# A sigmoid of one column behind the sines, and a new table of the order, in a recurrence with a gated long convolution

## The chip, the cores and the metric

The kernel runs on one core of one Trainium2 chip. The time is device microseconds of that core for one launch. Times of the kernel before are from three runs; engine times are from one profiled execution of it. Engines: TensorE (PE) multiplies matrices into PSUM, VectorE (DVE) and ScalarE (ACT) read PSUM and compute, GpSimd (POOL) computes on SBUF, SyncE (SP) issues all DMAs of this kernel from one queue. In this text an instruction takes "so many us" as the profile has it.

## The reference

Two stages, one behind the other (batch B = 4, sequence S = 6272, width D = 256, all float32):

```python
# stage 1: a gated linear recurrence along the sequence
sig = 1 / (1 + exp(-f_logit));  f = lower_bound + (1 - lower_bound) * sig
for t in range(S):
    h = f[:, t] * h + (1 - f[:, t]) * x[:, t];  y[:, t] = h
# stage 2: projection, circular convolution of one part along the sequence, gating
proj = y @ w_proj;  x1, x2, x3 = proj split in three of width D
x2_conv = irfft(rfft(x2, axis=1) * rfft(filter, axis=0), axis=1)
out = (x1 * x2_conv * x3) @ w_out
```

## The kernel before

The convolution of length 6272 = 49 * 128 is done by matrix products with small tables of sines and cosines, which the kernel makes itself.

**Prologue.** `prepare` (line 435) makes the tables: index patterns on POOL, arguments on DVE ("args", line 541), one sine over 520 columns on ACT ("sin", line 542), and copies of its parts into the tables D1, FT, VA, VB, ID. The filter (13 groups of up to four rows of 128 x 256, group 12 with one row) is loaded ("ff", line 604), cast ("fr", line 609), rotated on PE ("rot", line 615) and copied out of PSUM ("f2", line 618). Then for 16 units u come two first products ("FF1", line 630) with their copies "afs" (line 635), a small copy "mX" on POOL (line 639), the second product ("FF2", line 648), its scaled copy "hw" (line 653), and the store of the filter's spectrum to DRAM ("hst", line 657). "warm" (line 582) is a product of the identity that PE runs 24 times between the rotations; its results aren't used. "pad" (line 598, ACT in both orders) fills gaps of f2 with two copies. "W" (lines 477 to 487) scales and casts the weights.

**Recurrence** (`hgrn`, line 318), per batch in 13 chunks c of 512 steps (chunk 12 has 128): loads of f_logit and x, "sig" (the sigmoid, ACT, line 334), "u" (x times sigmoid, POOL, line 336), then for each half of the width: transposes "su" on PE (line 348), "f" (ACT line 361 or DVE line 363), "scan" (DVE, line 369) and, for the first half of the sequence, a copy "wrap" (line 377).

**Spectrum** (`spectrum`, line 827): `phase_p` (line 691) projects x2: 13 products "P" (line 700; group 12 has one row, the others four) and 13 copies "x2" out of PSUM to the tile X2, on ACT or DVE (line 703). All of them must be there before the transform "F1" (line 713) of any of the 16 units, whose copy is "A". "mini" and "zm" treat frequency zero; per unit follow "F2" (line 775), the load of the spectrum "H", two products with it per unit ("prod" on DVE straight from PSUM, called MUL in the table of the order, or a copy followed by "pm" on POOL, line 807), the inverse "I2" (line 817) and its copy "Th".

**Gate** (`gate`, line 384): products "x13" (line 397), copies "xs" and the product of the two, on DVE from PSUM (MUL, line 418) or on POOL ("z", line 427).

**Output** (`phase_o`, line 867): 13 groups of "I1" (PE, line 880), "y" (DVE, line 886), "proj" (PE, line 898), "o" (copy to SBUF, ACT or DVE, line 911) and "store" (SP, line 912). The tile ys has two halves, used in turn by even and odd groups.

The recurrence of batch b + 1 overlaps spectrum, gate and output of batch b.

**What sets the order.** The calls of `op` (line 77) only list operations, with the engines that may run each and an assumed length on each (its `cost`), for instance `either(n)` (line 296): 0.045 + n/1200 us on ACT and 0.07 + n/960 on DVE. The table ORDER (line 125) holds three characters per operation: its number, its engine and its PSUM bank. `emit` (line 108) walks the table and issues each operation on the engine named, so ORDER fixes the sequence on every engine and on the DMA queue, the engine of each operation that has a choice, and the banks. At run time each engine works through its own sequence, and semaphores hold it where data or a buffer isn't ready. SP is one such sequence: a load whose buffer isn't free holds back whatever stands behind it. ACT needs a table for the function it evaluates; the load of a table appears in the trace as an instruction of its own (ACT_TABLE_LOAD), ahead of the first activation that needs another table: at the start (line 280), before the sine (line 542) and before the first sigmoid (line 334).

Of the kernel before, what the change touches and what calls it, by code (L numbers as in the profile page):

```python
# [10 lines left out]
F32 = mybir.dt.float32  # L11
# [4 lines left out]
AF = mybir.ActivationFunctionType  # L16
# [45 lines left out]
class Plan:  # L62
# [63 lines left out]
    "A+gA2gAygA6gBCgBGgAAYAOYAgQAbQAiQAZQAaQAcQAeQAfQAdQAnQAhQAkQAqQAmQA3AABIACIA4QArSAPIAvSAzYARIA0SA7YA/IA1KAjUBAUA8WAp"  # L126
    "SBHYDngBWgBOgBKgAQAAXSAlTBegDmgBSgA5IBBMAxABIQBDYAtTBEUBJAA9GAUYBPIBQQBRAAVAAYCATIBFMBXYBagBigDpgDqgEBgD1gAoTADgD2gE"
    "NgDogECgEOgEZgEagElgAwTBLYAsTBMQBYUBZEAWIBTIBNIBfYBUSBgWBbIBcQBhGBjYASYAuUBVKBdABkUBlMDrADsYBoQBmUBpIBvSBwKBnEBtWEDA"
    "BuGBqYBxYAEYBrUB2SB4QBsMD3AByWDtUB5IB3KBzGB/QB9SB6YCAAB+CD4YCBYEEYB7WDxQDuMDvMB8GExgCCSDyIDzICDCEPACNUD5WCISD9QD6GCO"
    "MCJKD7OD+ACGUCHED/ICPSEFUCLWCQCCYSEGMEbACMGCWQEQYCKYCRYCZKCfWCSSCXAEnACTCEzAEHMEJQERUCgOEmgE7gEygCdWCeGEKICbSCcCEcYE"  # L130
    "SMELIETMCaYEoYAFgEVWEdQCmSEhUEWGE9AEXOEeACnCEfICoWEiEEpSCpGEjMCiQEqCCrWCjAErKChYCsGEtUE0YE1QEuMEvME8gFFgE2ACvSCtWAIY"
    "CwCCuGEIYCqYE+YAHYAJYEUYALYAMYAKYCxYFHAEMYE4SC2WCEgFPgAGgFGgFIYFZgFQgB0gFjgCFgFagCUgFkgE3ICyUE5CCzEC3OE6KE/QC9WC/UFC"
    "SFRADAEC+OFAIFbAFDKC4WDCUFBIC5GDDEC6YDBYFJWFEKDPQFKGFMUFLODQAFNEC7SJSQJTRC8CDIWDGSFOMJUAJVBDHKD0YFSYDJOJXQFtgFlAJZAA"
    "NYCVgFugDFgCkgDEgFTUFWSB1gFUMFVMDNWFXCFcYFmYEAYDOGDLQDMAFdWFYKDSUFeGFgQDWSDTEDKYDwYD8YDRYFfODYUFhAFvADXKDZEFnWDfSDdU"
    "FiIFoGDgCFwYEgYEkYEYYFqQFxSFpOFyKFzKDeEFrADiUJYWJcXF0SDjEDbUFsIF1KF2KJdQMtgJhRF+gEsYDcEDVgMugG2gF4gMVgMhgClgC0gDUgMi"
    "gF5gC1gDkgGkgDlgF3gGtgEwYJWYG/gMWgF6YF7YJauGQSGRCJePJfoJjJGSUGAWGBOGTEGUQMvAGVIGWSGGUGXCGHMGEWGIQMjAGJAMXAGFOGOUGCSG"
    "KQGLAGPMGDKGMUGNEJiWGYQJmXJnSGZIJkuJoHJpqDaYJlYMkYDhYGaQGbAGgWGeUGfEGcSGdCGlQGhOGnoF8WF9GJrUJsVJtMGpoGiSJwQJxUHIWJyA"
    "GjKGuQJzsG3SGyoGwoJuFHJGGzYGxYGmYGoYJvYGqYGrUG7qG5CHKWGsEJ1RJ2SJ3BJ4qHAUG4YGvYHLGHSgG0QG8YG6YHCsHEsHBYMYYJ6THOWG1AJ7"
    "SHPGJ8DJ9qHMQJ/UG9WKAVKBMHNAHTSHQQKEUG+GHXCHVqKCtHFYHWYHYYHDYKGEHGWKFTKJSHkgHbgH2UKHrHRIHHGHcWKLCHtgHlQIAgH3EHpAHguH"
    "euKDYHhYHdYHUYHZSHmYHnoHoYHqYJgYHfYH4UHaCH5EKKRKOXHiSH6UHjKKQHKMBHuWH7EH8QH9AHrSHwuHyuHsCH+QIBUH/IMZSIDEIFsIKQMaCMdW"  # L140
    "IOAMbKHvYJqYMwYKNYMeGHxYISgIJgICYHzYIEYH0UIGYIPYILYKPRH1EMfOIkSIHUITWIMoKRpIVuIlCIIEIcSIXGMlUMpQKTXMmMIgCIeCMqAIYYIU"
    "YINYIQSMrIMnMKVHKUWKYXKWuM5gF/gIbgIugM6gNFgIhYKIYIfYJ+YIdYNGgIWYI3gIRCIZSIvQIxoM7AKaHIaCImUInEKZXIoSKbvIpCKdWKeQIzoK"
    "fGIqUKiXIyYM8YIrEIiSKjRKkPKgoKlpIjCNHAIsUI4WItMI8uMxSM1QMyCIwYI9YI5YI6GI0YNIYKmYKnUKoVKsXKtWI7YMzKKpEM2AKqtKuHM9SM3I"
    "I1UJAgKvGM+CNBWKwYKXYNRgI2EM/KJBQJJgNSgKxUNJSKyVNCGJDAJFoKzENTANKCNDOK0tK2UI+QNNWI/ANLKK4ENOGNdgNegNngNogK3VK7QK8UK5"
    "tK9AJKSNPOK+sNfALAVLBQLFRJOqJbYJPYJEYKhYJ5YJLYJCYNUYLCFLDoJMCLEYJ0YKcYJGYNgYNVWLHBNWGNXOJHUJIENZSNhQLGUNaCNpANbKLKVN"
    "kWLLSLIsNiALMFNlGJNYNqYNjILNCJQULPTLQSJRENmOLRDLSqLJYK6YLOYKSYK/YLZUNxgNygN8gN7gLUQNrWNuSOGgOFgNsGNvCNQYNzAKrYMgYMcY"
    "N0YK1YLTYLaMLbULcELVILWQLjUNwKNtOLkMLXALeSRxWLfKN1QN9ARzGRyXN4UN2AN+YN3IR0HN5EOHAN6MLtSLlWLmGLgQLuKLoUN/WOCSLhALpMOA"
    "GOPgLdgOQgLYgLigOZgOagOBOLvQODCLwALqULrEM0YORAOEKOIYNMYM4YOSYNYYMsYMoYL3WL4OLyQOJSOMULzIONEL5WL0QOKCL6GL1AOOMOLKL8UL"
    "9MOTWR2QOWSR3ROUGObAOVOOXCR5BR4AOcYNcYNAYNEYL+UOYKOdWOgQOeGOfOMBSMGWOhAU1gLsgVBgLngU0gVMgLxgVNgL2gVAgL7gL/EOiIMCKMHO"
    "MAgO3QO4AOnUO1SOtWOrQOoEOuGOsAU2AOlUOmEVOAO2KO5WOjQOvSOwCO6OOxWOkIOzUO0MOyGOpSO7WMDQO8OOqCVCAO9SO+CMEIMLWPDUMMOPBQPE"  # L150
    "EO/SPCIMIWPACMQUPHQMRMPPSPJoMJGVPYU3YVDYR1YMFgPFUMNWPTCPGMPLoR7QMOGPnUR8TPoEPKYPQYPIYPMYPUYPNWPYYR6YR9IPRqPXQPZoPboP"
    "cYPSYPaYR+DPOGPfUPrSPhEPsCPVWSAQSBUSDMPjsSCAPpSPWGPdQPyWPqCPxgP6gP0uP2uPiYPgYP1YR/YP3YSFUPeAQDgMKgQfgQMgSEYPkYPtSSGV"
    "PuCPlQSIFP7SSHMPmAPvWPwOP/qSKVSLUP9CSMFU4WQVQSNsU5GQWAU6OP8YPzYP4SU8UU9MU+MQEQQIoP+YSJYP5CQNWQGAQRGQHYQJYQAYQBSQCCSP"
    "QSQXQXUSRAQZSSUQQYESWAQaCSSvQPuSVRSZXQbUSXpQSYSaQSeWSfRQcESbPSgOScoQFYQOYQQYSYYQKSQdWQeOQgUShBVEQVIWVZgQogVYgQisQLCQ"
# [24 lines left out]
    "9UgCKgFQglWf+EgDSgmGgHoi5Ui6Vi+QgEKgJogNSgRqgPqgQYizYgSYgIYi4YgKYi7Ei8FgGYi9YgOYgVWjAAdQUgXGdREgLQgMAi/WgnUgoEjDTjFD"
    "gYYgZujBugTQjESjGqgeYgaYgdUgfsggYgWYgbWgwSgUAghEgvggyqg0qgiYgzYgcGgpQg4ggqAjIUjJVgrWgjQjNSjOTjKEgsGjLtgkAjPKgtWg5Ugu"  # L180
# [12 lines left out]
def kernel(  # L193
# [33 lines left out]
    A = HA[:, A0:A0 + AW].rearrange("m (e r k) -> m e r k", r=2, k=64)  # L227
# [207 lines left out]
    def prepare(head, tmp):  # L435
# [165 lines left out]
        for g, r0 in enumerate(range(0, Q, 4)):  # L601
# [10 lines left out]
            def rotate(e, pb, r0=r0, rn=rn, fr=fr):  # L612
# [8 lines left out]
               w=[("f2", g)], src=rt)  # L621
# [360 lines left out]
```

## Time and profile before

| | |
|---|---|
| median of 3 runs | 461.38 us (461.21 to 462.36) |
| profiled execution, its own time | 462.5 us |
| its span, first to last instruction | 460.7 us |
| instructions | 14543 |
| moved by DMA | 119.04 MB, mean 258 GB/s |
| HBM read, written | 86.12 MB, 31.98 MB |
| granted PE clock | 0.995 of full speed on average |

The profile gives busy times per engine. Matmuls are pipelined and the ends of their records are modelled, so PE can be busy without being at its peak. In the lists, "[1.28 <-ACT Th L280]" behind an instruction means that its engine had been idle for 1.28 us before it and that the copy of line 280 into tile Th, on ACT, ended that wait. Tiles that share memory can appear under one name: the chunk buffers of the prologue under X, parts of the spectrum and staged output under HA or PP.

### The profile page before, as it was taken

To read this page: it belongs to the slowest core of one execution; us is meant where nothing else is said; L and a number is where in the kernel's file an instruction comes from. 1 tells how busy PE (TensorE), PEld (TensorE's weight loads), DVE (VectorE), ACT (ScalarE), POOL (GpSimd) and SP (SyncE) were. 2 spreads that over 40 slices of the span, in tenths; PEclk is the share of its full clock that TensorE was granted. 3 is DMA by queue.
4 is the path that set the end of the run, shared out by engine and by line. 5 is a ranking of instruction groups with operands and counts; after the bars stand their busy time and mean duration, and the time that the engine had idled before them with its cause. 6 is when DMAs were issued, how large, how long until landed. Compare 5 with 4: busy or idle time off the path is not lost.

```text
span 460.7 us, 14543 instructions
## 1 busy us (share of the span) xinstructions
PE 439.0 (95%) x6017; PEld 344.9 (75%) x6017; DVE 415.5 (90%) x466; ACT 388.8 (84%) x535; POOL 307.8 (67%) x287
## 2 busy tenths in 40 slices
PE   8889999999999999999989999999999999999995
PEld 7667767867766889877657889676768897776784
DVE  4779899899999996999989997999999989999874
ACT  5599998799998988899988968999998957888553
POOL 2559997258999753888997815889987604667500
PEclk9999999999999999999999999999999999999997
DMA  8989989865977799387947987568486831763167
GB/s 328 407 330 361 340 319 316 307 215 179 338 262 273 228 302 362 135 271 265 314 163 248 329 318 285 184 222 298 175 303 223 331 140 66 234 231 125 48 254 306
DMA packets 42562, 119.04 MB, mean 258 GB/s; under 512 B 4096, under 2 KB 5760, under 8 KB 42496
## 3 DMA queue, kind: packets, MB, share of 16 engines
q1 hardware_dynamic: 42496, 118.11, 71.5%
q8 instruction: 47, 0.77, 0.7%
q14 instruction: 19, 0.16, 0.1%
HBM read 86.12 MB, written 31.98 MB: 256 GB/s over the span
## 4 chain that ended last, share of the span: by engine, by line
PE 63%; DVE 12%; ACT 8%; POOL 6%; issue 5%; DMA 2%; DVEq 0%; ACTq 0%; POOLq 0%
PE PS L397 14%; PE PS L898 8%; PE PS L700 8%; PE PS L817 8%; PE PS L348 6%; PE PS L775 6%; PE PS L713 5%; DVE HA L369 4%; PE PS L880 4%; DVE ys L886 2%; DVE X L285 2%; PE PS L630 2%; POOL XT L336 2%; ACT HA L280 2%; DMA FL<-in_f_logit_dram 2%
## 5 line engine op out<-in xcount | busy, mean ns | idle before, releaser
L336 POOL TENSOR_TENSOR XT<-XT,FL 128x1024 f32<-128x1024 f32 (+1 forms) x47 | 105.0, 2238 | 53.4 <-DMA XT<-in_x_dram 32.0
L369 DVE TENSOR_TENSOR_SCAN HA<-fTs,HA,PS 128x512 f16<-128x512 f32 (+1 forms) x96 | 112.3, 1201 | 1.1 <-ACT fTs L361 0.2
L397 PE MATMUL PS<-HA,W 128*128 128x490 f16 (+1 forms) x416 | 101.7, 367 | 0.7 <-DVE ys L886 0.4
L807 POOL TENSOR_TENSOR PP<-HA,Hu 98x1008 f16<-98x1008 f16 x41 | 86.1, 2105 | 8.2 <-ACT HA L280 6.8
L280 ACT CAST HA<-PS 98x512 f16<-98x512 f32 (+1 forms) x105 | 84.0, 831 | 7.2 <-PE PS L713 3.9
L886 DVE TENSOR_TENSOR ys<-PS,zt 128x1024 fp32r<-128x1024 f32 (+1 forms) x52 | 58.7, 1154 | 8.2 <-PE PS L898 4.9
L798 DVE TENSOR_TENSOR PP<-PS,Hu 98x1008 f16<-98x1008 f32 x55 | 64.7, 1197 | 1.5 <-issue 0.7
L361 ACT ACTIVATE fTs<-PS,nomc 128x512 f32<-128x512 f32 (+1 forms) x89 | 58.9, 670 | 4.8 <-PE PS L348 2.8
L898 PE MATMUL PS<-Wo,ys 128*128 128x256 f32 x392 | 57.5, 293 | 2.8 <-DVE ys L886 2.8
L418 DVE TENSOR_TENSOR zt<-PS,XS 128x490 f16<-128x490 f32 (+1 forms) x83 | 52.9, 651 | 5.0 <-ACT XS L282 2.0
L817 PEld LDWEIGHTS <-PP 98*128 98x128 f16 x1024 | 48.9, 98 | 10.9 <-issue 2.6
L397 PEld LDWEIGHTS <-W 128*128 128x128 f16 x416 | 34.9, 97 | 28.8 <-issue 3.3
L898 PEld LDWEIGHTS PS<-Wo,ys 128*128 128x128 f32 x392 | 49.4, 189 | 7.0 <-DVE ys L886 3.9
L280 ACT CAST Th<-PS 128x784 f16<-128x784 f32 x61 | 49.8, 820 | 4.7 <-PE PS L817 3.5
L282 ACT ACTIVATE XS<-PS 128x490 f32<-128x490 f32 (+1 forms) x84 | 48.8, 584 | 5.6 <-PE PS L397 3.9
L817 PE MATMUL PS<-VA,PP 98*128 98x98 f16 x512 | 52.0, 207 | 0.3
L817 PE MATMUL PS<-VB,PP 98*128 98x98 f16 x512 | 51.7, 207 | 0.0
L334 ACT ACTIVATE FL<-FL 128x1024 f32<-128x1024 f32 (+1 forms) x47 | 47.4, 1008 | 3.2 <-DMA FL<-in_f_logit_dram 3.2
L700 PE MATMUL PS<-W,HA 128*128 128x256 f16 x392 | 44.1, 273 | 0.1
L700 PEld LDWEIGHTS <-HA 128*128 128x128 f16 x392 | 42.9, 142 | 1.1 <-issue 0.4
L348 PE MATMUL PS<-iden,FL 64*128 64x64 f32 x704 | 40.4, 230 | 2.7 <-ACT Th L280 1.3
L348 PEld LDWEIGHTS PS<-iden,FL 64*128 64x128 f32 x704 | 30.0, 138 | 16.4 <-DVE HA L369 2.5
(110 smaller groups left out, 766.4 us busy)
## 6 DMA issues: line engine op xcount, KB each, us to landing
FL<-in_f_logit_dram SPq DMA_DIRECT2D x43, 512.0 KB, 5.4
XT<-in_x_dram SPq DMA_DIRECT2D x43, 512.0 KB, 6.4
Hu<-H SPq DMA_DIRECT2D x39, 512.0 KB, 5.1
out_dram<-osb SPq DMA_DIRECT2D x24, 512.0 KB, 5.6
out_dram<-PP SPq DMA_DIRECT2D x16, 512.0 KB, 5.9
Hl<-H SPq DMA_DIRECT2D x13, 512.0 KB, 3.9
out_dram<-HA SPq DMA_DIRECT2D x8, 512.0 KB, 7.1
X<-in_moe_filter_fft_dram SPq DMA_DIRECT2D x7, 512.0 KB, 6.6
```

The lines of the kernel that those rows point to most:

```text
L280: nc.scalar.copy(dst, src)
L336: op("u", {"POOL": 0.1 + 0.553 * nb}, lambda e, xt=xt, ft=ft: nc.gpsimd.tensor_tensor(xt, xt, ft, op=AOP.mult), r=[("ft", k)], w=[("xt", k)])
L348: nc.tensor.transpose(bank(pb)[:, at[p] + j:at[p] + hn:nb], src[ps, j, cols], iden[ps, ps])
L361: nc.scalar.activation(fT, sT, AF.Identity, scale=by, bias=1.0)
L369: nc.vector.tensor_tensor_scan(h, fT, bank(pb)[:, 512 - hn:512 + hn], init, op0=AOP.mult, op1=AOP.add),
L397: nc.tensor.matmul(PS[:, p, 0:n], W13[:, kh, js], HA[:, HB[kh] + t0:HB[kh] + t0 + n], start=(kh == 0), stop=(kh == 1))
L700: nc.tensor.matmul(pp[:, r - r0, :], column(HB[kh], q_of(r)), W2[:, kh, :], start=(kh == 0), stop=(kh == 1))
L798: nc.vector.tensor_tensor(pr, px.unsqueeze(1).broadcast_to([TB, 2, UE, 63]), hh(), op=AOP.mult)
L807: nc.gpsimd.tensor_tensor(pr, spec[:, o, :, 1:64].unsqueeze(1).broadcast_to([TB, 2, UE, 63]), hh(), op=AOP.mult)
L817: nc.tensor.matmul(PS[:, ib + o, pr * TB:(pr + 1) * TB], PP[:TB, k, o, n, 2 * pr:2 * pr + 2, :], v[:TB], start=(n == 0), stop=(n == 1))
L886: nc.vector.tensor_tensor(late["ys"][:, yk, :, 0:rn * 128], PS[:, cb:cb + 2, 0:rn * 128], late["zt"][:].rearrange("p k r m -> p k (r m)") ...
L898: nc.tensor.matmul(po[:, i, :], late["ys"][:, yk, kh, i * 128:(i + 1) * 128], Wo[:, kh, :], start=(kh == 0), stop=(kh == 1))
```

## The change

**1. One operation is added** behind the sines, in `prepare`:

```diff
         op("sin", {"ACT": 0.5}, lambda e: act.activation(w, w, AF.Sin, scale=2.0 * math.pi / S),
            r=st, w=["v", "sin"], table="sin")
+        idle = tmp.tile([128, 1], F32, name="idle")
+        op("tbl", {"ACT": 1.4}, lambda e: act.activation(idle[:], iden[:, 0:1], AF.Sigmoid),
+           r=["iden"], w=["sin"], table="sigmoid")
         op("masks", {"DVE": 0.7, "POOL": 0.9}, masks, r=["cols"], w=["masks"])
```

It takes the sigmoid of one column of the identity into a tile that nobody reads. It writes the token "sin", which every "sig" reads, so all sigmoids are ordered behind it.

**2. All 63 lines of the table ORDER are new**, for 2419 operations instead of 2418. The dependences and the operations themselves are the same apart from "tbl". Of the 2418 operations 168 run on another engine, and 590 of the 763 that take PSUM have another bank. Decoded, these parts matter below (a number behind a name is the group, or the chunk; @ names the engine).

First operations on ACT:

```
before: fr1 sin pad f2_5 f2_2 f2_7 rest idw f2_9 f2_11 f2_10 sig0 afs ...
after:  fr1 sin fr2 f2_1 pad tbl f2_7 f2_4 idw fr11 f2_8 f2_10 sig0 sig1 ...
```

Sequence of the filter groups' loads on SP, and the engines of their casts:

```
before: 3 1 0 2 4 5 9 7 6 11 8 10 12    casts: ACT 1, DVE 4, POOL 8
after:  1 2 0 3 5 11 7 4 6 9 8 10 12    casts: ACT 3, DVE 3, POOL 7
```

POOL, from the middle of the prologue (W by its place among the seven weight operations, u by chunk, mX and wrap without number):

```
before: u5 mX u6 W2 wrap mX u7 W1 W3 wrap W5 W6 W4 mX wrap u8 mX mX wrap u9 W7 u10 u11 wrap ...
after:  u6 W3 mX W1 W4 mX u7 wrap u8 mX u9 mX u10 u11 mX wrap W5 mX W6 wrap wrap u12 ... W7 ...
        (W2 and two wraps are ACT's)
```

The projections (PE: P, in sequence), and how many of the 13 copies x2 each engine has:

```
batch 0 before: 8 9 0 10 11 3 2 4 7 1 5 6 12     after: 3 9 10 4 11 2 12 0 8 1 5 6 7
batch 1 before: 10 2 9 5 4 1 11 0 6 7 8 3 12     after: 10 7 1 12 5 9 3 0 8 6 2 4 11
batch 2 before: 8 10 6 12 9 3 5 2 0 1 7 11 4     after: 10 0 5 11 8 1 6 12 9 2 4 7 3
batch 3 before: 8 0 7 4 10 1 2 9 5 11 6 3 12     after: 2 1 8 6 0 7 10 11 5 9 4 12 3
x2 on ACT / DVE, batches 0 to 3   before: 6/7 8/5 5/8 6/7    after: 6/7 8/5 8/5 9/4
x2 of group 12                    before: DVE in all        after: ACT in batch 0, DVE in 1 to 3
```

In the projection of batch 2 three sigmoids of batch 3 stand among the x2 copies of ACT, in both orders.

Last operations of batch 3's output on PE and DVE:

```
before: ... proj10 I1_11 y9 proj9 y11 o9@DVE proj11 I1_12 y12 proj12 o12@DVE
after:  ... proj10 y9 proj9 I1_11 I1_12 y11 proj11 y12 proj12 o12@DVE   (o9@ACT)
stores at the end of SP, both: 7 10 8 9 11 12
```

Over the whole kernel, engines of the operations with a choice, where the counts differ by two or more:

| operation | before | after |
|---|---|---|
| x2 | ACT 25, DVE 27 | ACT 31, DVE 21 |
| afs | ACT 19, DVE 13 | ACT 23, DVE 9 |
| f | ACT 89, DVE 15 | ACT 84, DVE 20 |
| A | ACT 58, DVE 6 | ACT 56, DVE 8 |
| Th | ACT 61, DVE 3 | ACT 63, DVE 1 |
| o | ACT 47, DVE 5 | ACT 49, DVE 3 |
| prod | MUL 78, ACT 47, DVE 3 | MUL 76, ACT 50, DVE 2 |
| xs | MUL 83, ACT 104, DVE 21 | MUL 86, ACT 103, DVE 19 |
| wrap | POOL 48 | POOL 46, ACT 2 |
| fr | ACT 1, DVE 4, POOL 8 | ACT 3, DVE 3, POOL 7 |

More of the change, by code (lines that the diff above doesn't have):

```diff
@@ L130 @@
[L130 to L154, printed above, removed]
@@ L185 @@
[L185 to L188 removed]
+    "A3gA7gAzgA/gAAYAOYAVIA0YA4AAhQAcQABIACIAPIASYAQAAWIAjQAaQAbQAdQAfQAgQAeQA5QA1SAoUBAYAiUA2KA8ABHgBfgBPgAlUBBUArWAnWBD"
@@ L189 @@
+    "Wk4Ik0Sk5Qk1Ck9MlGSk2glCOk+Uk6AlDWlQQk/ElEGlHKlISlRIlJClaWlLUlMMlSSlTClNQlAgk7glFglOAlUglPglKglbOlVUlkWlWMlcSlXUllOl"
+    "YElfQlZglmWlnGldCloglgIlhUlpWluQlqOlrSlvIlwQlxIliElegljglsCltglyg"
 )
```

98 lines of the change are left out of this document (60 added, 38 removed).

## The prediction

> **What bounds the kernel now.** First the totals and the chain, then the span cut at the places where TensorE (PE) begins each batch's projection (line 700). In the second fence the columns are the stretch and its length, then the busy time of PE, of its weight loads, of DVE, ACT and POOL, with instruction counts, then PE's granted clock, the DMA share and GB/s.
>
> ```profile
> PE 439.0 (95%) x6017; PEld 344.9 (75%) x6017; DVE 415.5 (90%) x466; ACT 388.8 (84%) x535; POOL 307.8 (67%) x287
> PE 63%; DVE 12%; ACT 8%; POOL 6%; issue 5%; DMA 2%; DVEq 0%; ACTq 0%; POOLq 0%
> ```
> ```profile
> 0.00:25.20 25.20, 20.81 (x153) 16.78 (x154) 15.62 (x39) 14.05 (x17) 10.52 (x24) 1.00 0.95 367
> 25.20:76.40 51.20, 48.30 (x599) 36.84 (x599) 46.32 (x52) 48.51 (x66) 46.49 (x50) 1.00 0.92 333
> 76.40:171.30 94.90, 92.28 (x1374) 72.11 (x1373) 91.62 (x97) 86.85 (x123) 68.09 (x61) 1.00 0.76 264
> 171.30:271.90 100.60, 97.24 (x1427) 77.71 (x1427) 93.05 (x100) 90.35 (x127) 74.86 (x61) 1.00 0.76 262
> 271.90:371.30 99.40, 97.56 (x1434) 76.77 (x1432) 94.79 (x99) 89.59 (x127) 74.08 (x60) 1.00 0.71 257
> 371.30:460.70 89.40, 82.81 (x1040) 64.67 (x1038) 74.13 (x83) 59.48 (x79) 33.80 (x32) 0.97 0.48 177
> ```
>
> PE is busy nearly everywhere, and the new order gives it the same operations. What an order can win is its idle time: 4.4 us before 25.2, 2.9 to 76.4, then 2.6, 3.4 and 1.8 in the three middle stages, and 6.6 in the last, of which the final 3.5 are only the last copy and store: 21.7 us together. DVE is idle for only 3.3, 7.6 and 4.6 us of the middle stages, so PE waits mostly because several full engines wait for each other in turn; a gap closed at one place can open at another. Before 76.4 all four engines are full and the DMA engines too (0.95 and 0.92).
>
> **The change part by part.** Durations are from the profiled execution (462.5 us, its span 460.7 and 1.8 around it); it ran 1.1 us above the median of 461.38, and I carry the differences over to the median.
>
> *1. The table load.* ACT, early rows, and the chain where the load stands in it now:
>
> ```profile
> 9.05 1.95 ACT L280 CAST f<-iden 128x1920 fp32r<-128x1920 f32 x2
> 15.54 3.27 ACT L280 CAST f<-PS 128x1024 fp32r<-128x1024 f32 x3 [4.54 <-PE PS L615]
> ...
> 22.91 2.20 ACT L280 CAST f<-PS 128x1024 fp32r<-128x1024 f32 x2 [0.86 <-PE PS L615]
> 25.12 1.28 ACT L334 ACT_TABLE_LOAD   x1
> 26.41 1.06 ACT L334 ACTIVATE FL<-FL 128x1024 f32<-128x1024 f32 x1
> ```
> ```profile
> 26.41 0.98 ACT FL L334
> 27.39 0.56 ACT afs L280
> ```
> ```profile
> 27.56 2.40 POOL L336 TENSOR_TENSOR XT<-XT,FL 128x1024 f32<-128x1024 f32 x1 [3.39 <-ACT FL L334]
> ```
> ```profile
> L280 ACT CAST f<-iden 128x16 fp32r<-128x16 f32 x1 | 0.2, 193 | 0.0
> ```
>
> The load (1.28) now stands between the last filter copy and the first sigmoid, and the chain runs through that sigmoid to the afs copy behind it. POOL's first "u" (line 336) waited 3.39 us for the same sigmoid; after it POOL has 46.49 us of work in 51.2. The new operation moves the load to just after the "pad" copies on ACT (9.05 to 11.0), where ACT then waits 4.54 us. Its price there is 1.28 for the load and, by the nearest short copy (0.19), 0.2 for the sigmoid of one column. One filter cast and one more f2 copy come ahead of it as well, at 1.1 us each by the three copies of 15.54: 3.7 us in all, still inside the 4.54. If that cover is gone, what is queued behind is the f2 copy of group 7, and PE's rotations wait for its bank. Bounds: -1.28 (all of it on the path) to +1.5 (the old place had cover of its own and the new one has none). I take -1.0, near the first end, since two chains start behind the old load.
> The Trainium skill (ScalarE: Activation LUTs, What ACT_TABLE_LOAD costs) counts a further drain of about 1380 ns for every switch to another set, by which the saving would be up to 2.66 and the sum 1.4 us lower. The trace shows no such drain: the copy ends at 25.11, the load starts at 25.12, and the sigmoid at 26.41.
>
> *2. POOL's load before 76.4.* The chain in the middle of that stage:
>
> ```profile
> 54.15 2.75 POOL W L294 x3
> ...
> 57.60 2.35 POOL XT L336
> ...
> 60.00 0.47 PE PS L348 x8
> ```
>
> PE's transposes at 60.00 wait for a "u" on POOL that stood behind three weight scalings ("W"). In the new order two of the five scalings ahead of this "u" stand behind three later ones, a sixth and two wraps are ACT's. Bounds: 0 (ACT, busy 48.5 of 51.2, makes PE wait instead) to -2.9 (all PE idle time of the stage). I take -0.7.
>
> *3. The filter rotations before 25.2.* PE's waits there:
>
> ```profile
> 19.65 1.21 PE L615 MATMUL PS<-afs,rot 128*128 128x256 f32 x8 [0.82 <-POOL afs L292]
> 21.32 2.39 PE L615 MATMUL PS<-afs,rot 128*128 128x256 f32 x12 [0.47 <-DVE afs L285]
> ...
> 25.20 2.13 PE L630 MATMUL PS<-D1r,f 128*128 128x256 f32 x16 [0.92 <-ACT f L280]
> ```
>
> The new order loads the thirteen filter groups in another sequence and gives three casts to ACT, three to DVE, seven to POOL (one, four, eight now). The loads fill the DMA engines, so the last group can't land much sooner. Bounds: -2.2 (these three waits) to +1.0 (one ACT cast late). I take -0.4.
>
> *4. The end of each projection.* The copies x2 out of PSUM on DVE and ACT, and PE's waits behind the last of them:
>
> ```profile
> L285 DVE CAST X<-PS 128x1024 f16<-128x1024 f32 x23 | 27.5, 1229 | 7.9 <-PE PS L700 7.8
> L285 DVE CAST X<-PS 128x256 f16<-128x256 f32 x4 | 5.2, 1300 | 1.0 <-PE PS L700 1.0
> L280 ACT CAST X<-PS 128x1024 f16<-128x1024 f32 x25 | 24.7, 1014 | 11.0 <-PE PS L700 9.9 <-DVE XS L287 0.8 <-DVE ys L886 0.3
> ```
> ```profile
> 89.22 1.95 PE L713 MATMUL PS<-D,X 128*128 128x128 f16 x32 [0.70 <-DVE X L285]
> ```
> ```profile
> 183.79 0.61 PE L713 MATMUL PS<-D,X 128*128 128x128 f16 x8 [0.68 <-DVE X L285]
> ```
> ```profile
> 273.01 4.62 DVE X L285 x4
> ...
> 277.67 5.40 PE PS L700 x48
> ```
> ```profile
> 383.66 0.29 PE L880 MATMUL PS<-ID,Th 64*128 64x128 f16 x4 [0.52 <-DVE X L285]
> ```
>
> The quarter-sized group 12 costs DVE 1.30, as much as a full one, though the line that plans it (either(256)) says 0.34. The old order puts it last or nearly last on DVE in batches 0, 1 and 3; the new one has it in the middle, on ACT in batch 0, and only in batch 3 late. In batches 2 and 3 DVE hands three full copies each to ACT (8 to 5 and 7 to 4): 3.7 us off DVE and 3.0 onto ACT each time. The direct waits are 0.70, 0.68 and 0.52, and in batch 2 four copies stand in the chain in a row. Bounds: 0 (a loss here is rival B) to -3.1 (0.70, 0.68, 0.52 and one 1.23 of the four). I take -1.0.
>
> *5. The body of the batches.* Elsewhere about as many operations go from DVE to ACT as back, and loads, stores and banks are reordered. PE is idle for 7.8 us from 76.4 to 371.3, of which 0.70 and 0.68 are counted above. The longest wait is behind a load:
>
> ```profile
> 226.46 7.58 DMA FL<-in_f_logit_dram
> ```
> ```profile
> 235.88 0.46 PE L348 MATMUL PS<-iden,FL 64*128 64x64 f32 x8 [1.28 <-ACT Th L280]
> ```
>
> This f_logit load was issued only 7.58 us before the sigmoid that wanted it went on, and PE waited 1.28 us for a copy behind that sigmoid on ACT. Whether the new sequence on SP avoids such a case or makes one can't be read from it. Bounds: -6.4 (all the rest) to +3.0 (the added ACT work of one batch, unhidden). I take -0.6, a tenth of the gain's end, on DVE's lighter load.
>
> *6. The tail.* PE's last product and the last two stores on SP:
>
> ```profile
> 456.37 0.79 PE L898 MATMUL PS<-Wo,ys 128*128 128x256 f32 x2 [0.59 <-DVE ys L886]
> ```
> ```profile
> 456.65 1.34 SPq L910 DMA_DIRECT2D out_dram<-osb  x2
> ```
>
> Group 12's I1 now comes before group 11's product, so its y runs beside that product and the 0.59 goes. But the store of group 11 is issued first of the two and is four times as large; it moves little. Bounds: 0 to -0.6; I take -0.2.
>
> Sum: 1.0 + 0.7 + 0.4 + 1.0 + 0.6 + 0.2 = 3.9 us. Against it stands that an order which closes old gaps makes new ones that no row of the old trace can show. I keep three quarters, **-3.0 us**: 459.5 for the profiled execution, **458.4 us** on the median.
>
> **The rivals.**
>
> *A. No change that counts.* The start gains its 2.1 (parts 1 to 3), but later a load reaches its sigmoid late, as at 226.46. One more case of that size (1.28), and the gains of 4 to 6 taken up by new waits, give 461.4 - 2.1 + 1.3 = 460.6. For it: DMA shares of 0.7 to 0.9, and SP's sequence of stores and loads is all new. Against it: most loads wait for a buffer (the transposes), not for the DMA engines.
>
> *B. Slower: ACT becomes the bound.* The place is the projection of batch 2: eight copies at 1.014 and three sigmoids of 1.06 between them make 11.3 us for ACT while PE streams 98 products in 11.0 (48 take 5.40 in the row above). If ACT is not free when that stage starts, its added 3.0 us there count in full, and so do 0.6 in batch 3 (3.0 less two DVE copies of 1.2); the prologue keeps only part 1. 461.4 - 1.0 + 3.6 = 464.0. It decides from the point at which less than 3 us of ACT's idle time in a middle stage (8.0, 10.3 and 9.8) can be used. Against it: that idle time is larger than what is added.
>
> *C. Larger gain: DVE is the bound of the batches.* Then batch 2's 3.7 us off DVE come out in full, the other ends of the projections give 0.7, and with the 2.1 of the start and 0.2 of the tail the time is 461.4 - 6.7 = 454.7. For it: DVE idles least after PE in the middle stages, and the four DVE copies at 273.01. Against it: PE shows only 1.8 us idle in the stage of 271.9 to 371.3.
> A rule speaks against my reading of PE here: the Trainium skill (Perfetto Trace Analysis, Identifying the Most-Contended Engine) holds matmul busy time to be no good measure of the distance to the roofline and asks for the weight loads' share. By that rule 75% is the measure, PE's 21.7 idle microseconds are no limit, and C would be likelier than I make it.
>
> *D. The change doesn't do what it says:* a load of the table stays ahead of the first real sigmoid. Then part 1 falls: 459.4.
>
> **How the numbers follow.** The forecast 0.45, A 0.22, B 0.18, C 0.13, D 0.02. A measurement of this kernel tells about 0.3% (1.4 us) from no change: faster (forecast, C, D) 0.60, same (A) 0.22, slower (B) 0.18. The range goes from 455.0, nearly C's time, to 463.6, nearly B's; the outer halves of both are left out.
>
> **What would show it.** Part 1: a table load near 11 to 15 us, none at 25, and the first "u" on POOL before 27. Parts 2 and 3: the projection of batch 0 starts before 76.4, by about 2 us. Part 4: no DVE copy last before line 713, and no gap in the projection of batch 2. Part 5: the stages of batches 1 and 2 (100.6 and 99.4 long) shorter by under 1 us each. Part 6: 0.5 us or less. It is wrong if the start gains nothing, if ACT grows gaps on PE in batch 2, or if a single load or store holds ACT for several microseconds.

## The result, and the profile after

| | before | after |
|---|---|---|
| median, run beside each other | 461.29 us (461.04 to 462.36) | 456.30 us (455.94 to 457.66) |
| profiled execution, its own time | 462.5 us | 457.66 us |
| its span | 460.7 us | 455.5 us |

The ratio is 0.9893, 95% interval 0.9866 to 0.9919: 5.0 us faster (3.7 to 6.2). The forecast was 3.0 us, and the time on record, 458.4, is 2.1 us above what came. Both profiled executions are the longest of their kernel, so stages read from them are those of one execution each. One run of e9 below, 514.37 us long at a mean granted clock of 0.771, was slow and is left out of every figure. First the totals and the chain of the new kernel, then its span cut where PE begins the first products of the filter (23.43) and each batch's projection; columns as in the prediction.

```profile
PE 436.8 (96%) x6017; PEld 344.1 (76%) x6017; DVE 407.9 (90%) x456; ACT 392.8 (86%) x545; POOL 307.6 (68%) x287
...
PE 58%; DVE 14%; ACT 8%; issue 5%; DMA 5%; POOL 3%; SPq 0%; DVEq 0%; ACTq 0%; POOLq 0%
```
```profile
0.00:23.43 23.43, 20.87 (x153) 16.96 (x154) 16.44 (x37) 15.85 (x17) 11.35 (x28) 1.00 0.94 365
23.43:71.97 48.54, 47.46 (x599) 36.53 (x599) 46.77 (x53) 46.51 (x67) 45.02 (x48) 1.00 0.96 353
71.97:167.02 95.05, 92.41 (x1373) 72.05 (x1371) 91.30 (x95) 86.43 (x123) 69.29 (x60) 1.00 0.80 273
167.02:265.10 98.08, 96.55 (x1419) 76.87 (x1417) 91.52 (x97) 91.00 (x128) 73.33 (x60) 1.00 0.74 265
265.10:366.31 101.21, 97.91 (x1443) 77.81 (x1441) 93.83 (x99) 89.48 (x128) 75.97 (x61) 1.00 0.74 264
366.31:455.50 89.19, 81.62 (x1041) 63.86 (x1038) 68.03 (x77) 63.54 (x85) 32.65 (x31) 0.99 0.48 166
```

Read the lengths against those of before: 25.20 became 23.43 and 51.19 became 48.54; from there on 384.3 became 383.5. So, between these two executions, 4.4 of the 5.2 us by which the span shrank had been won when batch 0's projection began. PE's idle time (length less busy time) in the two stages of the start fell from 4.4 and 2.9 to 2.56 and 1.08. POOL's share of the chain fell from 6% to 3%, and that of transfers rose from 2% to 5%: the chain now goes through loads for longer.

The start, by rows: ACT early, POOL's first "u", and PE's last waits among the rotations.

```profile
11.08 1.97 ACT L280 CAST f<-iden 128x1920 fp32r<-128x1920 f32 x2
13.05 1.28 ACT L545 ACT_TABLE_LOAD   x1
14.35 0.20 ACT L545 ACTIVATE idle<-iden 128x1 f32<-128x1 f32 x1
16.92 2.24 ACT L280 CAST f<-PS 128x1024 fp32r<-128x1024 f32 x2 [2.37 <-PE PS L618]
...
23.10 3.22 ACT L334 ACTIVATE FL<-FL 128x1024 f32<-128x1024 f32 x3
```
```profile
24.26 2.41 POOL L336 TENSOR_TENSOR XT<-XT,FL 128x1024 f32<-128x1024 f32 x1 [2.11 <-ACT FL L334]
```
```profile
22.21 0.38 PE L618 MATMUL PS<-afs,rot 128*128 128x256 f32 x1 [0.17 <-POOL afs L292]
23.43 2.76 PE L633 MATMUL PS<-D1r,f 128*128 128x256 f32 x19 [0.84 <-DVE f L285]
```

The load of the table stands at 13.05, and behind the sigmoid of one column ACT still waits 2.37 us for PE: the cover holds. The first real sigmoid follows on a copy with no load ahead of it, and the first "u" begins at 24.26, where it began at 27.56. Of PE's three waits there (0.82, 0.47, 0.92) 0.17 and 0.84 are left.

PE's first rows, before and then after, show something that the lists of the change leave out:

```profile
1.36 8.28 PE L582 MATMUL PS<-iden 128*128 128x256 f16 x56 [1.36 <-POOL iden masks.py:199]
9.39 0.73 PE L615 MATMUL PS<-afs,rot 128*128 128x256 f32 x4
```
```profile
1.36 6.70 PE L585 MATMUL PS<-iden 128*128 128x256 f16 x36 [1.36 <-POOL iden masks.py:199]
7.82 1.19 PE L618 MATMUL PS<-afs,rot 128*128 128x256 f32 x8
```

Ahead of the first rotation the old order runs 14 of the 24 "warm" operations, 56 products whose results aren't used, and the new one 9, 36 products; the others stand between the rotations. The first rotation begins 1.57 us earlier. From there to "FF1" it takes 15.61 us instead of 15.81, so nearly all of what was won before "FF1" is there at the first rotation.

The batches: PE at the beginning of batch 0's transform and at the projection of batch 2, and the chain there.

```profile
84.00 1.95 PE L716 MATMUL PS<-D,X 128*128 128x128 f16 x32
...
90.00 1.05 PE L778 MATMUL PS<-HA,FT 64*128 64x256 f16 x16 [0.77 <-ACT X L282]
```
```profile
265.10 2.84 PE L703 MATMUL PS<-W,HA 128*128 128x256 f16 x24
267.70 1.19 PE L901 MATMUL PS<-Wo,ys 128*128 128x256 f32 x8
...
278.20 1.20 PE L901 MATMUL PS<-Wo,ys 128*128 128x256 f32 x8 [0.51 <-ACT X L280]
```
```profile
265.47 8.79 DMA FL<-in_f_logit_dram
...
274.33 1.06 ACT FL L334
```

The wait of the transform for a DVE copy of X2 is gone (84.00), but 6 us later PE waits 0.77 for a copy on ACT. In the projection of batch 2 the DVE copies have left the chain, and a load of f_logit, 8.79 us long, stands in it instead: the sigmoid behind it waits 0.69 us for it on ACT, the x2 copies queue behind the sigmoid, and PE waits 0.51 us for the last of them (278.20).

### The profile page after: what moved, and what is told of

It reads as the page before. It is cut to its first block, busy times and chain, and to the rows that moved or that the text cites. A ratio compares the mean times of both kernels' runs of the same rounds, so it can differ in the third digit from the quotient of the medians.

```text
span 455.5 us, 14537 instructions
## 1 busy us (share of the span) xinstructions
PE 436.8 (96%) x6017; PEld 344.1 (76%) x6017; DVE 407.9 (90%) x456; ACT 392.8 (86%) x545; POOL 307.6 (68%) x287
## 4 chain that ended last, share of the span: by engine, by line
PE 58%; DVE 14%; ACT 8%; issue 5%; DMA 5%; POOL 3%; SPq 0%; DVEq 0%; ACTq 0%; POOLq 0%
PE PS L397 14%; PE PS L820 8%; PE PS L703 7%; PE PS L901 7%; DVE HA L369 6%; PE PS L348 6%; PE PS L716 5%; PE PS L778 5%; DMA FL<-in_f_logit_dram 3%; PE PS L883 3%; DVE ys L889 3%; DMA XT<-in_x_dram 2%; DVE fTs L363 2%; PE PS L633 2%; DVE PP L801 2%
## 5 line engine op out<-in xcount | busy, mean ns | idle before, releaser
L397 PE MATMUL PS<-HA,W 128*128 128x490 f16 (+1 forms) x416 | 100.4, 367 | 0.3 <-ACT XS L282 0.2
L810 POOL TENSOR_TENSOR PP<-HA,Hu 98x1008 f16<-98x1008 f16 x43 | 90.2, 2106 | 4.3 <-ACT HA L280 2.0
L280 ACT CAST HA<-PS 128x1024 f16<-128x1024 f32 (+1 forms) x106 | 83.5, 821 | 4.9 <-PE PS L716 1.8
L801 DVE TENSOR_TENSOR PP<-PS,Hu 98x1008 f16<-98x1008 f32 x53 | 62.2, 1199 | 1.5 <-PE PS L820 0.7
L361 ACT ACTIVATE fTs<-PS,nomc 128x512 f32<-128x512 f32 (+1 forms) x84 | 55.8, 673 | 4.7 <-PE PS L348 2.3
L418 DVE TENSOR_TENSOR zt<-PS,XS 128x490 f16<-128x490 f32 (+1 forms) x86 | 54.7, 653 | 2.3 <-DVE XS L287 0.5
L280 ACT CAST Th<-PS 128x784 f16<-128x784 f32 x63 | 51.7, 823 | 4.0 <-PE PS L820 3.3
```

The source lines that it names most:

```text
L280: nc.scalar.copy(dst, src)
L361: nc.scalar.activation(fT, sT, AF.Identity, scale=by, bias=1.0)
L397: nc.tensor.matmul(PS[:, p, 0:n], W13[:, kh, js], HA[:, HB[kh] + t0:HB[kh] + t0 + n], start=(kh == 0), stop=(kh == 1))
L801: nc.vector.tensor_tensor(pr, px.unsqueeze(1).broadcast_to([TB, 2, UE, 63]), hh(), op=AOP.mult)
L810: nc.gpsimd.tensor_tensor(pr, spec[:, o, :, 1:64].unsqueeze(1).broadcast_to([TB, 2, UE, 63]), hh(), op=AOP.mult)
```

## The experiments

Each run gives the place of the stages; these are the first rows of "FF1" and of "P" on PE in its profile, and the span. The ratio is to the kernel before, run on the same chip.

| run | FF1 | P, batch 0 | 1 | 2 | 3 | span | ratio (95%) |
|---|---|---|---|---|---|---|---|
| before | 25.20 | 76.39 | 171.25 | 270.91 | 371.28 | 460.7 | |
| after | 23.43 | 71.97 | 167.02 | 265.10 | 366.31 | 455.5 | 0.9893 (0.9866 to 0.9919) |
| e1 new without the load | 23.70 | 73.24 | 167.62 | 265.68 | 365.99 | 455.1 | 0.9893 (0.9867 to 0.9919) |
| e2 old with the load | 25.03 | 75.50 | 170.57 | 269.22 | 370.87 | 460.3 | 0.9987 (0.9968 to 1.0006) |
| e3 new until P of batch 0 | 23.86 | 72.41 | 168.27 | 267.13 | 367.28 | 456.8 | 0.9935 (0.9913 to 0.9957) |
| e4 old until P of batch 0 | 24.67 | 75.14 | 175.00 | 273.35 | 372.73 | 461.9 | 1.0072 (1.0047 to 1.0096) |
| e5 new until FF1 | 23.73 | 74.19 | 169.05 | 268.74 | 368.84 | 458.2 | 0.9943 (0.9924 to 0.9963) |
| e6 old, W late | 25.54 | 75.58 | 170.42 | 269.53 | 369.46 | 458.8 | 0.9966 (0.9947 to 0.9984) |
| e7 old, new projections | 25.14 | 75.61 | 171.03 | 275.70 | 380.15 | 474.2 | 1.0279 (1.0255 to 1.0304) |
| e8 new until P of batch 2 | 23.82 | 72.34 | 167.05 | 265.10 | 365.13 | 454.8 | 0.9903 (0.9882 to 0.9924) |
| e9 new, small stores | 23.43 | 71.99 | 166.51 | 264.56 | 363.38 | 451.9 | 0.9814 (0.9787 to 0.9840) |
| e10 e1, small stores | 23.77 | 73.32 | 167.68 | 265.73 | 364.53 | 453.1 | 0.9837 (0.9810 to 0.9866) |
| e11 new until P of batch 1 | 23.72 | 72.29 | 169.15 | 270.34 | 370.27 | 459.8 | 0.9981 (0.9956 to 1.0006) |
| e12 old until P of batch 1 | 25.77 | 76.19 | 173.81 | 274.74 | 374.67 | 463.8 | 1.0065 (1.0043 to 1.0086) |

In e2 to e8, e11 and e12 the load is early too, and line numbers in all but e9 lie two to five below those of the new kernel.

### The load of the table, by itself

**e1** takes the added operation out of the new kernel; **e2** puts it into the old order, behind "pad".

```diff
e1, against the new kernel:
-        op("tbl", {"ACT": 1.4}, lambda e: act.activation(idle[:], iden[:, 0:1], AF.Sigmoid),
...
e2, in the old ORDER, operations of ACT:
-fr1 sin pad f2_5 ...
+fr1 sin pad tbl f2_5 ...
```

> The new order without the sigmoid of one column; the table load goes back to the first real sigmoid, near 23 us. Theory 'order': most of the gain at the start is the sequence itself, and the load costs up to 0.5 us: 456.3 to 456.8. Theory 'load': it stands on the path in full, 1.28 us plus what queues behind it: 457.3 to 457.8.

> The old order with the sigmoid of one column put behind the pad copies on ACT, nothing else. Theory 'load': 460.0 to 460.3 (1.0 to 1.3 below before). Theory 'order': the load was covered by PE's work, 460.9 to 461.4.

In e1 the load is back ahead of the first sigmoid. ACT, and POOL's first "u":

```profile
23.52 1.28 ACT L332 ACT_TABLE_LOAD   x1
24.82 2.96 ACT L332 ACTIVATE FL<-FL 128x1024 f32<-128x1024 f32 x3
```
```profile
25.96 2.38 POOL L334 TENSOR_TENSOR XT<-XT,FL 128x1024 f32<-128x1024 f32 x1 [3.53 <-ACT FL L332]
```

Batch 0's projection begins 1.27 us later than in the new kernel (73.24 and 71.97), about the length of the load, as expected. But that lead shrinks to 0.6 at batch 1's projection, is gone at batch 3's, and the two kernels have the same ratio. In the old order the load gives 0.89 at batch 0's projection, and 0.6 us of the time (-0.3 to 1.5), which isn't resolved.

These leads contain the place of "FF1", which differs by up to 1.1 us between runs of one order (24.67 to 25.77 in the five runs with the old start and the load). The stretch from "FF1" to batch 0's projection repeats within 0.05 us. By it the load is worth 1.0 in the new order (49.54 in e1, 48.54 in the new kernel) and 0.7 in the old (51.19 before, 50.47 in e2). So it is worth what was forecast where it stands. At the end nothing of it was measured, but each of the two ratios is uncertain by 0.26%, 1.2 us, so a microsecond can't be excluded there.

### Start and rest taken apart

**e3** follows the new order up to batch 0's projection and the old one from there, **e4** the other way round; **e5** follows the new one only until "FF1".

```diff
-ORDER = new
+e3: new until the first P of batch 0, then the operations left, in the old order and on the old engines
+e4: old until the first P of batch 0, then the operations left, in the new order and on the new engines
+e5: new until the first FF1, then old
```

> The new order up to the first product of batch 0's projection, the old order for all that is left. The start (projection of batch 0 at 71.97 in place of 76.39) carries the gain: 4.4 us, so about 456.9. Rival, the batches carry a good part of it: 458.5 or more.

> The old order (with the sigmoid of one column) up to the first product of batch 0's projection, the new order for the rest. If the start carries the gain, the rest gives 0.5 to 0.9: 460.4 to 460.8. Rival, the lighter load of DVE in batches 2 and 3 pays: 459.5 or less.

> The new order up to the first product FF1 (rotations of the filter, with the sigmoid of one column), the old order for all that is left. Theory 'two halves': FF1 starts near 23.5 in place of 25.2 and the rest of the start keeps its old length, so the projection of batch 0 starts near 74.0 and the time is 459.5 to 460.2. Rival, what is won before FF1 is waited away behind it because other engines are the bound there: projection at 75.3 or later, 461 or more.

The new start alone gives 3.0 us (2.0 to 4.0) of the time, less than the 4.4 that its expectation carried to the end; about 2.0 of the 5.0 are left for the rest of the order. Until "FF1" the new order wins 1.3 (e5 against e2: 23.73 and 25.03; over all runs with the load early, five with the old start and six with the new, 1.6 on average), and between "FF1" and the projection 1.9 (e3's stretch is 48.55 long, e5's 50.46). e4 lost, and in its profiled run it lost in batch 0's stage, 99.86 long. POOL there, and PE:

```profile
95.89 2.34 POOL L334 TENSOR_TENSOR XT<-XT,FL 128x1024 f32<-128x1024 f32 x1 [19.20 <-DMA XT<-in_x_dram]
98.19 0.54 POOL L781 TENSOR_TENSOR PP<-zp 98x32 f16<-98x32 f16 x2
```
```profile
98.58 0.22 PE L818 MATMUL PS<-VA,PP 98*128 98x98 f16 x1 [3.80 <-POOL PP L781]
```

An x load of batch 1 was issued only at 89.54, behind stores and loads of the spectrum in SP's sequence; the "u" that needs it held POOL for 19.20 us, small sums that PE needs queued behind it, and PE stood for 3.80. That says what such a joint costs, not what the rest of the new order is worth.

### POOL's weight scalings

**e6** moves two W and the wraps among them behind u11 in e2's order, as the new order has them.

```diff
-POOL: ... W5 W6 ... wrap u8 ... u11 ...
+POOL: ... u8 ... u11 ... W5 wrap W6 wrap ...
```

> The old order with the sigmoid of one column, and on POOL two weight scalings (the fifth and sixth of seven) with the two wraps that must follow them put behind the u of chunk 11, where the new order has these scalings; the other queues keep their order. Part 2 of the prediction: the projection of batch 0 starts 0.7 us or more before the 75.5 that the old order has with the sigmoid alone, 461.1 or less. Rival, POOL wasn't what counted there (DVE and ACT are as full): within 0.3 us of 75.5.

The chain before batch 0's projection, of e2 and then of e6:

```profile
53.26 2.74 POOL W L292 x3
...
56.71 2.36 POOL XT L334
...
59.11 0.47 PE PS L346 x8
```
```profile
62.87 0.97 ACT FL L332
...
63.90 1.80 POOL XT L334
...
66.27 1.23 POOL W L292 x2
67.50 1.64 POOL HA L290 x3
```

W left the place where it stood and came back 10 us later. "FF1" to projection is 0.4 shorter than in e2 (50.04 and 50.47; e4, e7 and e12, with the same order there, have 50.42 to 50.47). The projection is not earlier (75.58 and 75.50) only because "FF1", which stands ahead of the moved W, came 0.5 later in this run. The run's ratio is 0.2% below e2's, and their intervals overlap. In the new kernel no POOL work is in the chain of that stretch; it runs through DVE's scans:

```profile
63.06 0.73 DVE fTs L363
...
63.82 1.29 DVE HA L369
...
65.16 0.74 PE PS L633 x4
```

So W makes about 0.4 of the 1.9 us. Which other changes of that stretch do (W2 and two wraps on ACT, more "f" on DVE, the u ahead) was not taken apart.

### Projections and batches

**e7** gives the four projections of e2 the new sequence of P and the new engines of x2; 76 banks had to change with them. **e8** follows the new order until batch 2's projection, **e11** until batch 1's; **e12** is e11 the other way round.

```diff
-batch 2: P 8 10 6 12 9 3 5 2 0 1 7 11 4, x2 on ACT 5, on DVE 8
+batch 2: P 10 0 5 11 8 1 6 12 9 2 4 7 3, x2 on ACT 8, on DVE 5
...
```

> The old order with the sigmoid of one column, and in the four projections the sequence of products and copies and the engines of the copies of the new order, nothing else. Part 4 of the prediction: 1.0 us less than the old order with the sigmoid, 460.3 to 460.9. Rival, the waits at the ends of the projections come back elsewhere: 461.3 to 461.9.

> The new order up to the first product of batch 2's projection, the old order from there. The stage of batch 2 took 101.2 us in the new order's profile and 100.4 in the old one's. If that difference belongs to the order, this is 0.8 us faster than the new order, near 455.5. Rival, the stages' lengths vary that much by themselves and depend on what comes before: 456.3 or a little more.

> The new order up to the first product of batch 1's projection, the old order from there. With the change until batch 0's projection alone (e3) the time was 0.9935 of before, with the change until batch 2's projection (e8) 0.9903, whole 0.9893. If the rest of the gain comes from the body of batch 0 (output and recurrence beside it), this run gives 0.990 to 0.991 and batch 0's stage is 95.0 us long; if it comes from batch 1's stage, it gives 0.993 to 0.994 and the stage of batch 1 is 99 to 100 us long as in e3; if the rest of the order is worth nothing by itself, anything between 0.990 and 0.994 with stages that differ by no pattern.

> The old order (with the early sigmoid, as in e2) up to the first product of batch 1's projection, the new order from there: the other half of e11. If the new order of batches 1 to 3 is better by itself, its stages come out as in the new kernel (98.1, 101.2, 89.2) and the time is 1.2 us below e2, 0.996 of before; if it only suited the timing that the new start leaves (as the loss of e4 suggests, where it followed on the old start of batch 0), the time is that of e2 or above, 0.9987 or more, with a wait of POOL for an x load or a wait of PE at the joint.

e8 is as fast as the new kernel: the new order of batches 2 and 3 isn't needed for the gain. Nor is it 0.8 us faster, as its expectation had it if the longer stage of batch 2 in the new kernel belonged to the order. e11 and e12 lost at their joints, and e7 inside the projections. PE of e11 at the joint, then the stretches around it:

```profile
169.15 7.08 PE L701 MATMUL PS<-W,HA 128*128 128x256 f16 x39 [2.45 <-DVE ys L887]
```
```profile
167.00:168.00 1.00, 0.00 (x0) 0.00 (x0) 1.00 (x2) 0.00 (x0) 0.00 (x0) 0.90 1.02 418
...
169.00:170.00 1.00, 0.85 (x5) 0.67 (x5) 0.10 (x1) 0.00 (x0) 0.00 (x0) 0.50 1.14 320
...
173.00:174.00 1.00, 1.00 (x6) 0.75 (x5) 0.00 (x0) 0.77 (x1) 0.00 (x0) 0.50 1.02 414
...
175.00:176.00 1.00, 1.00 (x12) 1.00 (x11) 0.69 (x1) 0.51 (x1) 0.00 (x0) 1.00 1.03 422
```

The joint makes PE wait 2.45 us for a product on DVE that holds what the first P needs. In that wait the granted clock (third number from the end) falls to 0.50, and it stays there for 5 us after PE has work again: 6 products a microsecond instead of 12. The wait costs 2.45 and the clock, by estimate, about half of those 5 us again, some 5 us together; e11's stages of batches 0 and 1 are 4.9 longer than the new kernel's (1.8 and 3.1). e12 has the same at 173.81 (a wait of 2.14, then 0.50 for 3.3 us: by the same estimate 3.8), e4 after its 3.80 (5.5), and e7, whose stages of batches 1 to 3 are 6.0, 2.8 and 4.6 longer than e2's, in and right behind batch 1's projection, where it waits for copies x2 of both engines:

```profile
179.15 6.19 PE L701 MATMUL PS<-W,HA 128*128 128x256 f16 x40 [2.44 <-DVE X L283]
...
188.33 0.62 PE L714 MATMUL PS<-D,X 128*128 128x128 f16 x8 [1.10 <-ACT X L278]
```

So these runs don't measure parts 4 and 5: a piece of one order in the other fits badly, and the misfit costs more than the piece. (In e7 the copies and products before and behind the projection, and the banks, are still those of the old order.) What the new order is worth in the batches by itself was not isolated.

### Where the lead of the early load goes

The chain of the new kernel in the output of batch 0 has a load, with the work behind it, and PE waits there:

```profile
151.96 7.70 DMA XT<-in_x_dram
...
159.82 2.39 POOL XT L336
```
```profile
162.26 0.46 PE L348 MATMUL PS<-iden,XT 64*128 64x64 f32 x8 [0.70 <-POOL XT L336]
```

**e9** and **e10** are the new kernel and e1 with each store of the output cut to one of its four rows (three quarters of the output are left unwritten).

```diff
-                of, to = rows_of(*at, out[b].rearrange("(a r) d -> a r d", r=Q)[:, r0:r0 + rn, :], rn)
+                of, to = rows_of(*at, out[b].rearrange("(a r) d -> a r d", r=Q)[:, r0:r0 + 1, :], 1)
```

> The new order, but each store of the output writes one row of each group of four (it leaves three quarters of the output unwritten); everything else is as in the new kernel. To be read together with e10, the same edit without the early sigmoid. In the full kernels the early load gave 1.3 us at the start of batch 0's projection, 0.6 at batch 1's and nothing at batch 3's. Theory L (the lead is lost to loads that land late because stores and loads share the DMA queue: in the new kernel an x load took 7.70 us at 151.96 with the DMA engines full from 148 to 160): with the stores a quarter of their size that wait goes, the stretch from 160 to 170 has PE busy over 9.6 of 10 us, and this kernel keeps a lead over e10 of about 1.2 us at the start of the projections of batches 1 and 3 and about 0.25% in the time. Rival E (the lead is lost because DVE and ACT are full there anyway): the lead over e10 is gone by batch 3's projection also with small stores, and the times of e9 and e10 agree within their intervals. Both expect e9 to be faster than the new kernel by little (0 to 1%) as loads wait less.

> The new order without the early sigmoid, with the same quarter-sized stores as e9 (three quarters of the output are left unwritten). Theory L: batch 0's projection starts 1.2 us later than in e9, and so do those of batches 1 and 3, and the time is about 0.25% above e9's. Rival E: batch 0's projection starts 1.2 us later, batch 3's at the same time as in e9, and the times agree.

The lead of e9 over e10 is 1.33 at batch 0's projection, 1.17 at those of batches 1 and 2, 1.15 at batch 3's, and 1.2 at the end. The medians are 453.97 and 455.10; the runs lie between 453.93 and 454.17, and between 455.05 and 455.31, with no overlap. So 1.13 us, 0.25%, stay, and rival E, that full engines take the lead in any case, is out. Theory L's other half, that late loads take it in the full kernels, can be followed in the two profiled executions. The lead falls by 0.67 up to batch 1's projection, and PE's wait of 0.70 at 162.26, behind the x load, is in neither e1 nor e9. It falls by 0.90 within batch 2's stage, where from the projection's start to the transform the new kernel takes 14.15 and e1 13.58, by the f_logit load of 265.47; e1 waits there for no load, and neither does e9. Whether the usual run loses the lead in this way isn't shown, since the two full kernels' times don't tell 1 us apart. The stretches from 150 to 170, of the new kernel, then of e9:

```profile
150.00:160.00 10.00, 9.87 (x168) 8.84 (x167) 10.00 (x10) 9.01 (x12) 6.47 (x7) 1.00 0.99 314
160.00:170.00 10.00, 8.96 (x133) 7.85 (x133) 8.68 (x9) 8.51 (x14) 5.17 (x6) 1.00 0.72 252
```
```profile
150.00:160.00 10.00, 9.87 (x168) 8.84 (x167) 10.00 (x10) 9.01 (x12) 8.06 (x7) 1.00 0.69 190
160.00:170.00 10.00, 9.54 (x140) 8.48 (x139) 9.05 (x10) 9.27 (x14) 3.70 (x6) 1.00 0.74 220
```

The DMA share between 150 and 160 (last number but one) falls from 0.99 to 0.69, POOL does 1.6 us more there, and PE 0.58 more in the next ten (9.54; the expectation had said over 9.6). That e9 would be up to 1% faster than the new kernel held too (0.9814 against 0.9893). In the profiles most of it is batch 2's stage, 101.21 in the new kernel and 98.82 in e9, where the load at 265.47 stands.

## Why the prediction was right, and where it was not

*The sign* was right, and it came from where the reasons for it stood: the start. *The size* was 2.0 us short: in the two profiled executions the start gave 4.4 instead of 2.1, the rest 0.8 instead of 1.8. These two errors have opposite signs, so it is partly luck that the total came as near as it did. In e1, which has no lead of the load to lose, the rest gives 2.4 (381.9 us from batch 0's projection, 384.3 before). By times, e3 leaves about 2.0 for the rest, so the 0.8 is the least certain of these figures.

*1. The load, -1.0.* Right at its place (0.7 in the old order, 1.0 in the new, by the stretch from "FF1"), and with the cover that was named: ACT's wait of 2.37. That it is below 1.28 in both bears out that no further drain lies on the path. What isn't borne out is the step from there to the end: in the profiled execution of the full kernel the microsecond is lost to late loads.

*2. W on POOL, -0.7.* The whole stretch from "FF1" gained 2.65, of which the load has about 0.7 to 1.0 and the new order 1.9. The bound (0 to -2.9) held. The named cause carried a part: e6 moved W and won 0.4 there.

*3. The rotations, -0.4.* The term that was mis-sized most: 1.5 without the early load (e1, 23.70 against 25.20), 1.3 with it (e5 against e2). The step reasoned from the loads and from three waits among the rotations, but most of the gain arose elsewhere. It was there at the first rotation: PE came to it through 36 unused products instead of 56. In the old order the cast for it was done at 7.19, on ACT, and it began at 9.39; in all six runs with that start "FF1" follows the first rotation by 15.78 to 15.81 us, while the first rotation lies between 8.86 and 9.98. The waits among the rotations did shrink, but the stretch did not (15.81 and 15.61), since 20 more unused products stand in it now. In the eight runs with the new start "FF1" follows POOL's first cast of a filter group instead, by 16.28 to 16.45 us, and that cast waits for a load (6.98 to 7.55): the loads, which the step named, set the next limit. No run changed the place of these products alone, so this is read from rows. The prediction looked for gains in PE's idle time; ahead of the first rotation PE was busy, but with products whose results nobody reads (what they do for PE's clock was not tested).

*4. Ends of the projections, -1.0.* The mechanism was there: in batches 0, 1 and 3 no copy on DVE holds up the transform any more, and it begins 0.80, 0.18 and 0.57 us sooner after the projection's start (12.03 instead of 12.83 in batch 0). To the first I2 all of it is gone in batch 0 (91.44 and 95.82: 19.47 instead of 19.43), and 0.43 and 0.47 are left in batches 1 and 3. In batch 2 there was no gap of PE to close: a product of the output fills the place in both orders (267.70, and 273.66 before). Its transform begins 0.34 later, behind the late load; in e1, which doesn't wait for that load, 0.23 sooner.

*5. The body, -0.6.* The three stages from batch 0's projection to batch 3's together went from 294.9 to 294.3, in which parts 4 and 5 lie: 0.6 where 1.6 was forecast. In e1 they take 292.8, 2.1 less than before. So a size near the forecast is there, and the load's lead was paid back out of it. Where it comes from was not isolated. The prediction cut batch 2's stage at 271.90, 1.0 us behind the first row of its projection; by the first rows the stages of batches 1 and 2 were 99.66 and 100.37 long and became 98.08 and 101.21. That batch 2's is 0.8 longer isn't the new order's doing: e1 has the same order there and takes 100.31.

*6. The tail, -0.2.* 89.42 became 89.19, as forecast. PE at the end:

```profile
446.09 1.18 PE L901 MATMUL PS<-Wo,ys 128*128 128x256 f32 x8 [0.33 <-DVE ys L889]
...
449.30 1.42 PE L901 MATMUL PS<-Wo,ys 128*128 128x256 f32 x10 [1.36 <-DVE ys L889]
```

The wait of 0.59 ahead of group 12's product went, as the step said, and one of 0.33 came. In the old tail the granted clock had also fallen to 0.50, at 456.1, ahead of that product; in the new one it stays at 1.00 until PE's last product is done.

*The discount.* Keeping three quarters of the sum was meant for new gaps. They came (parts 1, 4 and 6 each show one), and in the profiled execution they took about what the load had won; but the sum itself was too small at the start, by part 3 and the stretch of part 2.

*The rivals.* A named the right mechanism, a late load, and in the profiled execution it took back the load's microsecond; the start was too large for it to decide. B didn't happen: ACT's busy time in batch 2's stage is 89.48, no more than before (90.14, from 270.91 on). One of its signs shows, PE's wait of 0.51 behind a copy on ACT at 278.20, but by a late load, and e1 doesn't have it. C's time (454.7) is nearer to what came than the forecast's, yet not by its mechanism: DVE's busy time in batch 2's stage fell by 1.95 only (95.78 to 93.83), and the stage, where DVE's relief was to come out in full, got longer. D fell with the row at 13.05. On the rule from the Trainium skill (Perfetto Trace Analysis, Identifying the Most-Contended Engine) that busy matmuls are a poor measure, e11 agrees, though the skill's reason is pipelining and here it is the clock: between 170 and 174 PE is busy in full at half the work.

## What to carry to other kernels

A gain found on the path of one stage is worth its size up to the end only if nothing between paces the work by itself; here a queue of loads and stores can take it back, and with the transfers made small in both of two kernels the gain lasted. An engine that shows no wait may still be in the way: ask whether the work that it is busy with is needed there. Where single runs are compared, find a stretch that repeats, since a start that differs between runs of one order can hide or feign an effect. A schedule searched as a whole can't be tested by transplanting pieces of it: joints that stopped PE for 2 to 4 us cost, by the estimate above, 4 to 5.5.

## What was not expected of the hardware

- **The clock of PE falls around a short wait.** In e11 it was granted at 0.50 from about 1.1 us into the wait of 2.45 (0.90 on average from 167 to 168) until 174.6, 5.5 us after the work had come back. In e12, e7 (batch 1) and e4 it fell 0.1, 0.3 and 1.4 us after the work had come back, and stayed down for 3.3 to 3.4 us; e11's 6.8 is twice that. The Trainium skill (TensorE: Matmul & The Clock Gate, What's actually happening) states half the clock after an idle window of about 3.4 us, and the full one after as much sustained work. The half agrees, and so does the time until the full clock in e12, e7 and e4. The condition doesn't: waits of 2.14 (e12), 2.44 (e7) and 2.45 (e11) were enough, and in the 3.4 us before the fall PE had been busy for 1.20, 0.95 and 1.85 us. At the end of the old order waits of 1.37 and 0.59 were enough together (1.70 busy in the 3.4 us before 456.1). A wait of 1.36 us in the new kernel's last stage left the clock at 1.00.
- **The spread of the runs went with the size of the stores.** With full stores the runs of one kernel differ by 1.7 to 1.9 us (455.94 to 457.66, 456.24 to 458.15), with small ones by 0.24 and 0.26.
- **A single wait in an in-order engine reaches far:** 19.20 us of POOL in e4, for one load of 512 KB that SP issued only at 89.54.
